# Two output stores cut into 119 and 9 rows, in place of own tiles for the halves of each w_in block and an earlier near half of the first mask

## The chip, the cores and the metric

The kernel runs on one core of one Trainium2 chip. The metric is the device time of one execution in microseconds (us), from the median of three runs. The core's engines are called PE (matrix products, with PEld for its weight loads), DVE (vector), ACT (activation), POOL (general purpose) and SP (which only issues DMAs). DMAs issued on one queue are carried out by 16 DMA engines side by side.

## The reference

Two stages follow each other, both with a recurrence over 768 steps of each of 4 sequences. The first is gated linear attention with 8 heads of width 48; its output, heads side by side (384 wide), is the input of the second, a gated state space block with inner width 512.

```python
for t in range(S):                       # first stage, per batch and head
    state = alpha[t][:, None] * state + outer(k[t], v[t])
    y[t] = q[t] @ state
x = heads_side_by_side(y)                # (4, 768, 384)

proj = x @ w_in                          # second stage; w_in is 384 x 1024
val, gate = proj[..., :512], proj[..., 512:]
for t in range(S):
    h = exp(A_log) * h + val[:, t];  ys[:, t] = h
out = (silu(gate) * ys) @ w_out          # w_out is 512 x 384
```

The weights and `A_log` come as 64-bit floats and are turned into 32-bit floats on the chip; the other inputs are 32-bit floats.

## The kernel before

The work is cut into 12 groups of 256 steps (3 groups for each of the 4 sequences), each of two chunks of 128. In a chunk the recurrence of the first stage becomes products of matrices: with running products of alpha (a scan on DVE, `products`, for the first group `chunk_products`), q is multiplied by the running product and k by its inverse (`Z`), the scores are k by q (`scores`), they are masked to the causal half (`masks`), multiplied with v (`values`), and what came from earlier chunks is added (`carried`, with the state that `state` sums up from the transposed keys of `keys`). `join` puts the heads side by side as `xT` by DMAs. The second stage projects a group in four blocks (`project`: for each block of 128 inner rows, three products for the value and three for the gate), runs the recurrence as a scan on DVE (`hidden`), gates it (`gate`, ACT and POOL), and multiplies with w_out (`output`).

The order is written out by hand: every engine runs its instructions in the order in which the program text gives them, and a framework adds the waits, by what each tile is written and read by. The group loop interleaves the second stage of group n with the first stage of group n+1 and the scans of group n+2; the first two groups have a longer prologue of their own (lines 849 to 982).

These places matter here:

- **Masks.** The scores of a chunk lie in two PSUM banks, one for even heads ("near") and one for odd heads ("far"). `masks_near` (L734) multiplies the near half with the mask on DVE; `masks_far` copies the far half on ACT (L729) and masks the copy on POOL (L730). The pair of banks comes in turn from one tile that spans two banks (`both`, b23) and from two tiles of one bank each (b4, b5). In b23, whichever of L734 and L729 stands second in the program waits for the first one; in b4 and b5 neither waits for the other.
- **Prologue.** `masks(0, 0, True)` puts the near half of the first chunk's mask ahead of the copy of the far half. Later, for group 1, the order on PE is scores(1,0), keys(1,0), scores(1,1), keys(1,1), state(1,0), values. The pair b23 goes to scores(1,0), the pair b4, b5 to scores(1,1).
- **Weights.** A w_in block is loaded by two DMAs (value half, gate half), each into its own tile `bits_in[i][vg]`. `low_word` (ACT, L531) turns the low 32-bit words into integers, `high_word` (DVE, L540 and L542) puts together the high words, and `word_sum` (POOL, L548) adds both into `w_in[i][vg]`, half by half. `check_w` (DVE, L559) finds the largest and smallest high word of each half, for a check whose outcome `fast` returns; if it is bad, a general kernel runs after the fast one.
- **Last stores.** In the last group both output tiles are copied from PSUM by DVE (L841) and stored by SP (L842), 128 rows of 1536 bytes each. After them the program branches over the general kernel (L1058) and ends.

Of the kernel before, what the change touches and what calls it, by code (L numbers as in the profile page):

```python
# [10 lines left out]
FP32 = mybir.dt.float32  # L11
U8 = mybir.dt.uint8
U32 = mybir.dt.uint32
AF = mybir.ActivationFunctionType
ALU = mybir.AluOpType
# [322 lines left out]
I32 = mybir.dt.int32  # L338
# [8 lines left out]
def fast(  # L347
# [18 lines left out]
    nc = tc.nc  # L366
    B, H, S, D = q.shape
    DM = H * D
    DI = moe_A_log.shape[0]
    C = 128  # L370
    G = 2
    GC = G * C
    NG = S // GC
    N = B * NG
    NT = GC // 32
    NK = DM // C
    NI = DI // C
# [6 lines left out]
    const = pool("const", 1)  # L384
# [3 lines left out]
    p4 = pool("p4", 4)  # L388
# [4 lines left out]
    next_mm, next_pair = itertools.cycle("016"), itertools.cycle((0, 1))  # L393
# [52 lines left out]
                             in_=v[b, :, ds(g * GC + c * C, C), :].rearrange("h p d -> p h d"))  # L446


    w_in = [[const.tile([C, NK, C], FP32, name=f"w_in{i}{vg}") for vg in range(2)] for i in range(NI)]
    w_out = const.tile([C, NI, DM], FP32, name="w_out")  # L450
    NW = NI + 2
    bits_in = [[const.tile([C, NK, C, 2], U32, name=f"bits_in{i}{vg}") for vg in range(2)] for i in range(NI)]
    bits_out = const.tile([C, NI, DM, 2], U32, name="bits_out")

    def load_w_in(i, engine):
        for vg in range(2):
            engine.dma_start(out=bits_in[i][vg].rearrange("p kk n two -> p kk (n two)"),
                             in_=moe_w_in.bitcast(U32)[:, ds(2 * (vg * DI + i * C), 2 * C)]
                             .rearrange("(kk p) n -> p kk n", p=C))

# [28 lines left out]
    inv_c = [inv[:, ds(c * 4 * C, 4 * C + 1)] for c in range(G)]  # L489
    ratio = const.tile([C, N, 4], FP32, name="ratio")  # L490
    above = const.tile([C, N], FP32, name="above")
    wmin = const.tile([C, NI + NW], FP32, name="wmin")
    wmax = const.tile([C, NI + NW], FP32, name="wmax")
    ok = const.tile([C, 4], FP32, name="ok")
    flag = const.tile([1, 1], I32, name="flag")

# [19 lines left out]


    def unit(i):

        if i < NI:  # L520
            return list(zip(bits_in[i], w_in[i]))
        return [(bits_out[:, 2 * (i - NI) + r, None], w_out[:, 2 * (i - NI) + r, None]) for r in range(2)]

    wrs = {}

    def low_word(i):
        wrs[i] = []
        for bits, w in unit(i):
            _, x, y = w.shape
            wr = p4.tile([C, x, y], I32, tag=f"wr{len(wrs[i])}", name="wr")  # L530
            nc.scalar.activation(wr, bits[..., 0], AF.Copy, scale=2.0 ** -29)  # L531
            wrs[i].append(wr)

    def high_word(i, banks):

        for (bits, w), bank in zip(unit(i), banks):
            _, a, n = w.shape
            x = bank[:, 0:NK] if a == NK else bank.rearrange("p h n -> p (h n)")[:, None, 0:n]
            h = bits[..., 1]
            nc.vector.tensor_scalar(out=x, in0=h, scalar1=3, scalar2=0x3FFFFFFF,  # L540
                                    op0=ALU.logical_shift_left, op1=ALU.bitwise_and)
            nc.vector.scalar_tensor_tensor(out=w.bitcast(U32), in0=h, scalar=0xC0000000, in1=x,  # L542
                                           op0=ALU.bitwise_and, op1=ALU.bitwise_or)

    def word_sum(i):
        for (_, w), wr in zip(unit(i), wrs.pop(i)):
            w = w.bitcast(I32)
            nc.gpsimd.tensor_tensor(out=w, in0=w, in1=wr, op=ALU.add)  # L548

    def check_w(i):  # L550
        his = []
        if i < NI:
            his = [t.rearrange("p kk n two -> p (kk n) two")[:, :, 1].bitcast(FP32) for t in bits_in[i]]
        else:
            his = [bits_out[:, ds(2 * (i - NI), 2)].rearrange("p cc n two -> p (cc n) two")[:, :, 1].bitcast(FP32)]
        for half, hi in enumerate(his):
            j = 2 * i + half if i < NI else NI + i
            for t, op in ((wmax, ALU.max), (wmin, ALU.min)):
                nc.vector.tensor_reduce(out=t[:, j:j + 1], in_=hi, axis=mybir.AxisListType.X, op=op,  # L559
                                        apply_absolute_value=True)  # L560
                if half == len(his) - 1:
                    yield

    def check_end():
        red = const.tile([C, 4], FP32, name="red")
# [56 lines left out]
    def chunk_products(c, al):  # L622

        by_place = lambda t: t.rearrange("p (h n) -> p h n", h=4)
        al_0, flat = by_place(al)[:, :, 0], last_c[c].rearrange("p h n -> p (h n)")[:, 0:4 * C]
        prod, inv = prod_c[c], inv_c[c]
        nc.vector.tensor_mul(first_c[:, :, 0], al_0, ends[-1])  # L627
        nc.vector.memset(al_0, 0.0)
        nc.vector.tensor_tensor_scan(out=prod, data0=al, data1=first_c.rearrange("p h n -> p (h n)"),
                                     initial=0.0, op0=ALU.mult, op1=ALU.max)  # L630
        yield
        end, inv_end = by_place(prod)[:, :, C - 1], last_c[c][:, 1:5, 0]
        ends.append(end)
        if c:
            nc.vector.tensor_scalar(out=ratio[:, 0], in0=end, scalar1=1.0 / FIRST_PRODUCT, scalar2=None,
                                    op0=ALU.mult)
        nc.vector.reciprocal(inv_end, end)
        nc.vector.tensor_copy(out=inv[:, 4 * C:], in_=last_c[c][:, 4, 0:1])
        nc.vector.tensor_tensor_scan(out=inv[:, 0:4 * C][:, ::-1], data0=al[:, ::-1], data1=flat[:, ::-1],
                                     initial=last_c[c][:, 4, 0:1], op0=ALU.mult, op1=ALU.add)  # L640
        yield
# [56 lines left out]
    def keys(m, c, b=None):  # L698

        if (m % NG) * G + c == NG * G - 1:  # L700
            return
        tp = mm(4, C, b=b)
        for p in range(4):
            nc.tensor.transpose(tp[:, p, :], Zs[m][:, p, 1, ds(c * C, C)], ident)
        nc.scalar.activation(ktms[c].rearrange("p a i d -> p a (i d)"), tp, AF.Copy)

    def scores(m, c):
        Z = Zs[m]
        cols = ds(c * C, C)
        sc = pair_of(4, C)  # L710
        for p in range(4):
            for i in range(2):
                rows = ds(64 * i, D)
                nc.tensor.matmul(sc[i][:, p, :], Z[rows, p, 1, cols], Z[rows, p, 0, cols], start=True, stop=True)  # L714
        As[m, c] = p2.tile([C, 2, 4, C], FP32, tag="A", name="A"), sc

    def masks(m, c, near_first=False):
        if near_first:
            masks_near(m, c)
        masks_far(m, c)  # L720
        if not near_first:
            masks_near(m, c)

    def mask_all():
        return mask[:, None, :].to_broadcast([C, 4, C])
# [1 line left out]
    def masks_far(m, c):  # L727
        A, sc = As[m, c]
        nc.scalar.activation(A[:, 1], sc[1], AF.Copy)  # L729
        nc.gpsimd.tensor_mul(A[:, 1], A[:, 1], mask_all())  # L730

    def masks_near(m, c):
        A, sc = As[m, c]
        nc.vector.tensor_mul(A[:, 0], sc[0], mask_all())  # L734
# [59 lines left out]
    def project(n, cc):  # L794
        if cc == 0:
            fs[n] = p1.tile([C, NI, GC], FP32, tag="f", name="f")
        xT = xTs[n]
        pv, pg = mm(GC), mm(GC)
        for vg, pj in enumerate((pv, pg)):
            for kk in range(NK):  # L800
                nc.tensor.matmul(pj, w_in[cc][vg][:, kk, :], xT[:, kk, :],  # L801
                                 start=(kk == 0), stop=(kk == NK - 1))
        return pv, pg

# [19 lines left out]
    def output(n):  # L824
        b, g = divmod(n, NG)
        os = [mm(DM) for c in range(G)]

        def part(ccs):
            for c in range(G):
                for cc in ccs:  # L830
                    nc.tensor.matmul(os[c], fs[n][:, cc, ds(c * C, C)], w_out[:, cc, :],  # L831
                                     start=(cc == 0), stop=(cc == NI - 1))

        def finish():
            part(range(split, NI))
            for c in range(G):
                o_sb = p3.tile([C, DM], FP32, tag="o_sb", name="o_sb")
                if n < N - 1:
                    nc.scalar.activation(o_sb, os[c], AF.Copy)  # L839
                else:  # L840
                    nc.vector.tensor_copy(out=o_sb, in_=os[c])  # L841
                nc.sync.dma_start(out=out[b, ds(g * GC + c * C, C), :], in_=o_sb)  # L842

        split = NI - 1 if n else NI // 2
        part(range(split))
        return finish
# [47 lines left out]
    qk[0]()  # L894
    qk[1]()
    scores(0, 0)
    steps = chunk_products(1, als[1].rearrange("p h n -> p (h n)"))
    next(steps)
    masks(0, 0, True)
    keys(0, 0, "6")  # L900
    al = both()
    for c in range(G):
        turned("a", 1, c, al.rearrange("p b (h n) -> p (b h) n", n=GC)[:, :, ds(c * C, C)])
# [28 lines left out]
    qk.append(natural_qk(1, "q", 1, mm(4, C, b="6")))  # L932
    next(steps)
    qk[0]()
    scores(1, 0)
    masks_far(1, 0)
    keys(1, 0, "0")
    qk[1]()
    qk[2]()
    masks_near(1, 0)  # L940
    scores(1, 1)
    masks(1, 1)
    keys(1, 1, "1")
    next(next_pair)
    low_word(0)
    state(1, 0)
    values(1, 0)
# [142 lines left out]
```

## Time and profile before

| | us |
|---|---|
| median of 3 runs (295.08 to 296.49) | 295.79 |
| the profiled execution's own time | 295.08 |
| its span, first to last instruction | 293.4 |
| PE busy in the span | 281.5 |
| DVE busy | 224.7 |
| POOL busy | 116.4 |
| ACT busy | 100.3 |

Times in profile lines are microseconds from the start of the span unless marked ns. In a timeline line the first number is the start, the second the busy time, then engine, line of the kernel, operation, what is written and read, sizes, the number of merged instructions, and in brackets the idle time of the engine ahead of it and what ended that. "SPq" marks DMA issues by SP. A group line that merges instructions gives the time from its first start to its last end. In DMA answers a row of 40 digits or of 40 GB/s values cuts the window into 40 equal slices. On PE each 32-bit product shows as two records, so the 24 products of a projection are 48.

### The profile page before, as it was taken

Reading aid. Unit: us, or ns where it says so; the run is one execution under the profiler, and the core shown is the slowest. Engines: PE = TensorE matmul, PEld = TensorE weight load, DVE = VectorE, ACT = ScalarE, POOL = GpSimd, SP = SyncE. Lnnn points to the kernel's source line nnn. Section 1 sums busy time; section 2 is a strip of 40 time slices with the busy share of each in tenths; the row PEclk is TensorE's granted clock in tenths of the full one; section 3 lists DMA queues with packets and bytes.
Section 4 is the critical chain, followed back from the end, with each engine's and each line's share of the span. In section 5 each row is a group of like instructions: output and inputs, shape, how many; then the busy total and the mean of one; then the engine's idle time right before and its main releaser. Section 6 shows DMA issues by size and latency. Waiting matters only on the chain. (4 is left out here: it accounts for less than half of the span.)

```text
span 293.4 us, 6146 instructions
## 1 busy us (share of the span) xinstructions
PE 281.5 (96%) x2345; PEld 226.5 (77%) x2345; DVE 224.7 (77%) x277; ACT 100.3 (34%) x226; POOL 116.4 (40%) x116
## 2 busy tenths in 40 slices
PE   7699999999999999999999999999999999999992
PEld 6578877885886896886886886886886886886870
DVE  5998887899996799799699699699699695312211
ACT  2457634432432432432432431431531531431110
POOL 7138791374642612642613513542523423401110
PEclk9999999999999999999999999999999999999998
DMA  9999969999992991991991991891891401101101
GB/s 129 163 162 298 366 125 169 233 264 212 237 207 65 236 167 34 246 187 35 244 175 34 241 185 34 219 202 37 210 213 39 108 11 35 54 11 31 55 4 63
DMA packets 71231, 42.09 MB, mean 143 GB/s; under 512 B 47492, under 2 KB 70536, under 8 KB 71192
## 3 DMA queue, kind: packets, MB, share of 16 engines
q1 hardware_dynamic: 69760, 40.96, 67.3%
q0 software_dynamic: 384, 0.44, 0.7%
q8 instruction: 20, 0.33, 0.6%
q10 hardware_dynamic: 1048, 0.20, 0.4%
q14 instruction: 19, 0.16, 0.2%
HBM read 33.33 MB, written 4.72 MB: 130 GB/s over the span
## 5 line engine op out<-in xcount | busy, mean ns | idle before, releaser
L801 PE MATMUL mm<-xT,w_in 128*128 128x256 f32 x576 | 131.0, 383 | 0.0
L801 PEld LDWEIGHTS mm<-xT,w_in 128*128 128x128 f32 x576 | 107.4, 190 | 17.8 <-issue 1.9
L817 POOL TENSOR_TENSOR f<-sg,hh 128x256 f32<-128x256 f32 x48 | 62.0, 1291 | 94.9 <-DVE hh L809 45.7
L831 PE MATMUL mm<-w_out,f 128*128 128x384 f32 x192 | 64.6, 487 | 0.7 <-DVE hh L809 0.6
L730 POOL TENSOR_TENSOR A<-A,mask 128x512 f32<-128x512 f32 x24 | 30.1, 1271 | 66.7 <-ACT A L729 66.7
L831 PEld LDWEIGHTS mm<-w_out,f 128*128 128x128 f32 x192 | 36.2, 190 | 24.1 <-DVE hh L809 1.3
L816 ACT ACTIVATE sg<-mm 128x256 f32<-128x256 f32 x48 | 18.4, 383 | 91.6 <-PE mm L801 89.5
L809 DVE TENSOR_TENSOR_SCAN hh<-a_dec,hh,mm 128x256 f32<-128x256 f32 x32 | 23.2, 726 | 20.2 <-PE mm L801 20.1
L734 DVE TENSOR_TENSOR A<-pair,mask 128x512 f32<-128x512 f32 x24 | 16.1, 688 | 26.6 <-ACT A L729 16.9
L661 DVE TENSOR_TENSOR_SCAN prod<-aT,first 128x1024 f32<-128x1024 f32 x10 | 27.5, 2750 | 0.1
L682 DVE TENSOR_TENSOR_SCAN inv<-aT,last 128x1025 f32<-128x1025 f32 x10 | 25.5, 2548 | 0.3
L839 ACT ACTIVATE o_sb<-mm 128x384 f32<-128x384 f32 x22 | 10.8, 490 | 43.8 <-PE mm L831 43.8
L714 PE MATMUL pair<-Z 48*128 48x128 f32 x384 | 25.2, 279 | 0.5 <-DVE first L627 0.2
L714 PEld LDWEIGHTS pair<-Z 48*128 48x128 f32 x384 | 22.6, 187 | 2.9 <-issue 2.1
L745 PE MATMUL pair<-A,v 128*64 128x128 f32 x352 | 21.3, 274 | 0.0
L745 PEld LDWEIGHTS pair<-A,v 128*64 128x64 f32 x352 | 19.1, 137 | 0.0
L647 DVE STREAM_TRANSPOSE aT<-raw_a 128x1024 f32<-128x1024 f32 x9 | 18.4, 2042 | 0.8 <-DMA raw_a<-in_alpha_dram 0.8
L647 DVE STREAM_TRANSPOSE Z<-raw_q 128x1024 f32<-128x1024 f32 x9 | 18.2, 2020 | 0.0
L647 DVE STREAM_TRANSPOSE Z<-raw_k 128x1024 f32<-128x1024 f32 x9 | 18.2, 2020 | 0.0
L729 ACT ACTIVATE A<-pair 128x512 f32<-128x512 f32 x24 | 13.3, 596 | 6.5 <-PE pair L714 3.5
L766 PEld LDWEIGHTS st<-v,ktm 128*64 128x64 f32 x320 | 11.4, 137 | 3.5 <-issue 3.5
L618 ACT ACTIVATE junk<-raw_a,minus 128x1024 bf16<-128x1024 f32 (+1 forms) x12 | 13.1, 1091 | 0.1
(119 smaller groups left out, 252.1 us busy)
## 6 DMA issues: line engine op xcount, KB each, us to landing
raw_k<-in_k_dram SPq DMA_DIRECT2D x24, 192.0 KB, 5.3
raw_q<-in_q_dram SPq DMA_DIRECT2D x24, 192.0 KB, 6.4
v<-in_v_dram SPq DMA_DIRECT2D x24, 192.0 KB, 6.4
out_dram<-o_sb SPq DMA_DIRECT2D x24, 192.0 KB, 1.9
raw_a<-in_alpha_dram SPq DMA_DIRECT2D x23, 192.0 KB, 4.2
raw_a<-in_alpha_dram SPq DMA_DIRECT2D x18, 176.0 KB, 4.3
raw_k<-in_k_dram SPq DMA_DIRECT2D x18, 176.0 KB, 5.7
raw_q<-in_q_dram SPq DMA_DIRECT2D x18, 176.0 KB, 6.7
```

The lines of the kernel that those rows point to most:

```text
L647: nc.vector.transpose(out=to.rearrange("p h (c j) -> p h j c", j=NT), in_=raw_bufs[m % NR][name].rearrange("p h (j d) -> p h j d", d=D)[:, ...
L661: nc.vector.tensor_tensor_scan(out=prod, data0=al, data1=first.rearrange("p h n -> p (h n)"), initial=0.0, op0=ALU.mult, op1=ALU.max)
L682: nc.vector.tensor_tensor_scan(out=inv[:, ::-1], data0=aT[:, ::-1], data1=lasts[:, 0:4 * GC + 1][:, ::-1], initial=0.0, op0=ALU.mult, op1= ...
L714: nc.tensor.matmul(sc[i][:, p, :], Z[rows, p, 1, cols], Z[rows, p, 0, cols], start=True, stop=True)
L730: nc.gpsimd.tensor_mul(A[:, 1], A[:, 1], mask_all())
L734: nc.vector.tensor_mul(A[:, 0], sc[0], mask_all())
L745: nc.tensor.matmul(ys[m][i][ds(64 * s, 64), e, ds(c * C, C)], v_sb[:, c, 2 * p + i, :], A[:, i, p, :], start=(c == 0 and e == 0), stop=Fal ...
L801: nc.tensor.matmul(pj, w_in[cc][vg][:, kk, :], xT[:, kk, :], start=(kk == 0), stop=(kk == NK - 1))
L809: nc.vector.tensor_tensor_scan(out=hh, data0=a_dec[:, cc:cc + 1].to_broadcast([C, GC]), data1=pv, initial=prev_h[cc][:, GC - 1:GC] if n % ...
L816: nc.scalar.activation(sg, pg, AF.Silu)
L817: return lambda: nc.gpsimd.tensor_mul(fs[n][:, cc, :], sg, hhs.pop((n, cc)))
L831: nc.tensor.matmul(os[c], fs[n][:, cc, ds(c * C, C)], w_out[:, cc, :], start=(cc == 0), stop=(cc == NI - 1))
```

## The change

Four edits, all in `fast`.

1. `w_in[i]` and `bits_in[i]` become one tile for both halves of a block, with the half as the third dimension. `low_word` is one ACT instruction of 128x768 in place of two of 128x384 (it then waits for both DMAs of the block), as it is for the two parts of w_out. `high_word` and `word_sum` stay two halves, but the DVE instruction for the first half now waits for both DMAs too. `check_w` makes two reductions of 128x768 for each block in place of four of 128x384.
2. In chunk (0,0) the copy of the far half stands ahead of the near half in the program. In the built program L734 of this chunk then waits for L729 (before, L729 waited for L734), and the transposes of alpha of group 1 (L592), which reuse the pair of banks, wait for L734 in place of L729. The order of instructions on each single engine is the same here.
3. In group 1 the pair of banks is swapped (`next(next_pair)` stands earlier), and keys(1,0) moves behind scores(1,1): PE has scores(1,0), scores(1,1), keys(1,0), keys(1,1); ACT has both copies of far halves, then both copies of keys. Now L734 of chunk (1,1), in place of that of (1,0), waits for its L729. No DMA is moved.
4. Each of the two stores of the last group becomes two, of 119 rows and of 9 rows, issued one after the other on SP.

```diff
-    w_in = [[const.tile([C, NK, C], FP32, ...) for vg in range(2)] for i in range(NI)]
+    w_in = [const.tile([C, NK, 2, C], FP32, name=f"w_in{i}") for i in range(NI)]
-    bits_in = [[const.tile([C, NK, C, 2], U32, ...) for vg in range(2)] for i in range(NI)]
+    bits_in = [const.tile([C, NK, 2, C, 2], U32, name=f"bits_in{i}") for i in range(NI)]
...
     def low_word(i):
-        wrs[i] = []
-        for bits, w in unit(i):
-            _, x, y = w.shape
-            wr = p4.tile([C, x, y], I32, tag=f"wr{len(wrs[i])}", name="wr")
-            nc.scalar.activation(wr, bits[..., 0], AF.Copy, scale=2.0 ** -29)
-            wrs[i].append(wr)
+        lo, _, w = unit(i)
+        _, x, y, z = w.shape
+        wrs[i] = p4.tile([C, x, y, z], I32, tag="wr", name="wr")
+        nc.scalar.activation(wrs[i], lo, AF.Copy, scale=2.0 ** -29)
...
     def word_sum(i):
-        for (_, w), wr in zip(unit(i), wrs.pop(i)):
-            w = w.bitcast(I32)
-            nc.gpsimd.tensor_tensor(out=w, in0=w, in1=wr, op=ALU.add)
+        w, r = unit(i)[2].bitcast(I32), wrs.pop(i)
+        for half in range(2):
+            x, y = (t[:, :, half] if i < NI else t[:, half] for t in (w, r))
+            nc.gpsimd.tensor_tensor(out=x, in0=x, in1=y, op=ALU.add)
...
-                nc.sync.dma_start(out=out[b, ds(g * GC + c * C, C), :], in_=o_sb)
+                rows = [C] if n < N - 1 else [119, 9]
+                for i, size in enumerate(rows):
+                    at = sum(rows[:i])
+                    nc.sync.dma_start(out=out[b, ds(g * GC + c * C + at, size), :], in_=o_sb[ds(at, size)])
...
     scores(0, 0)
+    masks_far(0, 0)
+    keys(0, 0, "6")
     steps = chunk_products(1, als[1].rearrange("p h n -> p (h n)"))
     next(steps)
-    masks(0, 0, True)
-    keys(0, 0, "6")
+    masks_near(0, 0)
...
     qk[0]()
+    next(next_pair)
     scores(1, 0)
     masks_far(1, 0)
-    keys(1, 0, "0")
     qk[1]()
     qk[2]()
     masks_near(1, 0)
     scores(1, 1)
     masks(1, 1)
-    keys(1, 1, "1")
-    next(next_pair)
+    keys(1, 0, "1")
+    keys(1, 1, "0")
     low_word(0)
     state(1, 0)
```

## The prediction

> **What bounds the kernel now.** I read the page first, then busy time by stage, then the timelines of the prologue and of the stretch after it, engine by engine, and last the end of the span with its DMAs. The page's busy row and two stages of the stage table:
>
> ```profile
> PE 281.5 (96%) x2345; PEld 226.5 (77%) x2345; DVE 224.7 (77%) x277; ACT 100.3 (34%) x226; POOL 116.4 (40%) x116
> ...
> 47.00:75.00 28.00, 27.32 (x239) 22.07 (x238) 26.76 (x29) 10.32 (x23) 12.12 (x14) 1.00 1.10 227
> 75.00:97.00 22.00, 22.00 (x185) 17.81 (x184) 17.42 (x17) 7.59 (x19) 9.71 (x6) 1.00 0.76 168
> 252.00:274.00 22.00, 22.00 (x164) 17.48 (x160) 5.59 (x17) 5.09 (x13) 5.40 (x6) 1.00 0.10 32
> ```
>
> From 75 us on PE is busy for all of each stage (22.00 of 22.00, at full clock, 1.00), so a delay of PE that still stands at 75 us stands at the end, and nothing that only DVE, ACT or POOL save after 75 us counts. Before 75 us PE has small gaps, and after its last product (287.5) come 5.9 us of copying, storing and closing. The change touches these two places only. First the prologue, timelines of DVE, ACT and PE:
>
> ```profile
> 12.26 0.69 DVE L734 TENSOR_TENSOR A<-pair,mask 128x512 f32<-128x512 f32 x1
> 12.98 0.60 ACT L729 ACTIVATE A<-pair 128x512 f32<-128x512 f32 x1 [3.04 <-DVE A L734]
> ...
> 23.47 0.68 DVE L607 TENSOR_TENSOR Z<-mm,prod 128x512 f32<-128x512 f32 x1
> 24.99 0.69 DVE L734 TENSOR_TENSOR A<-pair,mask 128x512 f32<-128x512 f32 x1 [0.84 <-ACT A L729]
> ...
> 24.78 1.16 PE L714 MATMUL pair<-Z 48*128 48x128 f32 x16
> 26.45 0.67 PE L766 MATMUL st<-v,ktm 128*64 128x48 f32 x16
> 30.29 0.92 PE L801 MATMUL mm<-xT,w_in 128*128 128x256 f32 x3
> ```
>
> From 12.26 to 24.15 DVE runs back to back, and PE's scores follow its Z products; PE's first projection starts at 30.29. Then the last gap of PE:
>
> ```profile
> 55.52 2.06 DVE L647 STREAM_TRANSPOSE aT<-raw_a 128x1024 f32<-128x1024 f32 x1 [0.82 <-DMA raw_a<-in_alpha_dram]
> 67.56 0.68 DVE L809 TENSOR_TENSOR_SCAN hh<-a_dec,hh,mm 128x256 f32<-128x256 f32 x1
> ...
> 65.56 2.10 PE L831 MATMUL mm<-w_out,f 128*128 128x384 f32 x6
> 68.30 3.49 PE L831 MATMUL mm<-w_out,f 128*128 128x384 f32 x10 [0.64 <-DVE hh L809]
> ```
>
> At 55.52 DVE waits for a load, then runs back to back until the scan at 67.56, and PE's second output product waits for that scan's bank. This gap is set by a DMA and DVE, not by PE. Now the end:
>
> ```profile
> 287.49 1.03 SPq L842 DMA_DIRECT2D out_dram<-o_sb  x2
> ...
> DMA  0000000559872988501110000000010200000000
> DMA packets 293, 0.44 MB, mean 69 GB/s; under 512 B 32, under 2 KB 288, under 8 KB 288
> q1 hardware_dynamic: 288, 0.39, 17.4%
> q14 instruction: 4, 0.03, 1.7%
> q8 instruction: 1, 0.02, 1.4%
> out_dram<-o_sb SPq DMA_DIRECT2D x2, 192.0 KB, 3.3
> ...
> DMA packets 20, 0.03 MB, mean 17 GB/s; under 512 B 3, under 2 KB 20, under 8 KB 20
> ...
> DMA to landing us min/median/max: 1.9/1.9/6.5
> ```
>
> In the window 287 to 293.4 there are 256 rows and 32 small packets (one closing count for each of 16 engines and each store). Two bursts, then a trickle: from 290.0 on (second packet line) only 17 rows and 3 counts are left, so at most two engines are late. Code is fetched in the same stretch (q8, q14). The two stores land after 3.3 us where the median store takes 1.9. A row takes 0.174 x 16 x 6.4 / 288 = 0.062 us.
>
> **The change, part by part.** The sum is made against the profiled execution, 295.08 (span 293.4 and 1.7 around it); the median of the runs is 0.71 above it.
>
> *First mask.* ACT's L729 can start once the scores are there: PE's L714 of 16 records takes 1.16 from 10.99, so 12.15, and in the prologue ACT follows PE by 0.10: 12.25 to 12.85. L734 then starts at 12.88 in place of 12.26: +0.62 on DVE, and its queue behind it is full: the scans, the Z products of chunk (0,1) and of group 1. PE's transposes (L592, 13.68) wait for L734's end, 13.57, in place of L729's, 13.58: no change. The scores after them follow DVE, and scores(1,0) starts at 23.72 in place of 23.10. The far half is finished on POOL 0.7 earlier, which nobody waits for.
>
> *Keys behind the second scores.* Scores(1,1) now stands right behind scores(1,0), and waits for the last Z product, 24.15 + 0.62 = 24.77: it starts at 24.92 (24.78 before). With L714 taking 1.09 to the next start, keys(1,0) runs 26.01 to 26.67, ACT copies it 26.76 to 27.36, and state(1,0) starts at 27.43 in place of 26.45. So PE is +0.98 late, of it 0.36 from this move; the rest of its chain (0.51 + 1.76 + 0.55 + 1.02 to L801) is unchanged: first projection 31.27. DVE's near masks, 25.0 and 26.8, are ready in time; the words of block 0 on POOL end at about 29.9 and 31.0, needed at 31.3 and 32.6.
>
> *Merged tiles.* One 128x768 low word, by the nearest row (L618, 128x768) 0.93, where two of 0.56 took 1.03. The first sum starts at most 0.4 later than its half alone would, behind slack of over 1 us. Waiting for both halves' DMAs costs up to 1.13 us for block 2 (ACT waited until 30.92 and 32.05), but DVE takes that block only behind the scan at 32.87. The join of group 1 slips 0.4 on ACT; its DMAs queue behind the loads anyway, as they land at 39 to 41 us and are needed at 47. POOL with rows of 128 apart: the nearest pair, L921 (such rows) 1.28 against L730 1.27, so nothing. The reductions: 16 x 0.53 become 8 x 0.93, DVE saves 1.0 us after 75 us, under PE: nothing.
>
> *What is late next.* PE carries +0.98 from 30.3 to 66.5. DVE's chain from 55.5 does not: it waits there for a load that queues behind other loads, and with +0.98 its previous scan ends at 55.67, 0.15 after that load. L734 of group 2 then waits for a later L729 (57.5 to 58.1), but before, L658 took 0.99 beside POOL's mask, which moves to 58.15; the scan at 67.56 comes no later. PE reaches its second output product at 66.54 + 1.94 = 68.48, and no longer waits, against 68.30: 0.8 of the 0.98 is taken up. At 72.7 another 0.1 goes (scores there waited for DVE's Z). Front: +0.1, bounded by -0.4 (a PE delay of only half the size with a DVE chain that gets shorter) and by +1.0 (nothing taken up).
>
> *Last stores.* SP issues four times 0.33 in place of two; the second 119 rows can be issued at 288.22, as before (288.19). How many engines 119 rows use, the trace does not show. It shows equal shares: 128 rows on 16 engines, and on ACT's queue 1048 packets, which is 1024 rows of a load with its 16 counts and a 4-row transfer with 4. Equal shares of 119 (7 x 17) mean 7 engines with 17 rows, or one; of 9, nine engines or three. I take 7 and 9, and the same engines each time, which is the slower way. Data starts 0.84 after issue: 17 rows from 288.32 end at 289.37, the next 9 at 289.43, the second 17 at 290.5, the last 9 at 290.55. An undisturbed store has 1.9 - 0.84 - 8 x 0.062 = 0.56 from last row to landing: 291.1, against 288.19 + 3.2 = 291.4. That is -0.3 if the late engines are not among the seven. If one is, it has 36 rows where it had 16: +1.2. If 119 rows go over 16 engines, 0 to +0.2. All on one engine: 238 x 0.062, +12, excluded by me as no transfer here does so.
>
> The Trainium skill, page "DMA: Bandwidth & Descriptors", section "Why a DMA increments its semaphore by 16 and not by 1", says that such a transfer uses the largest number of engines up to 16 that divides its rows, and the lowest-numbered ones; the counts above agree as far as they go, and which numbers they are, no row shows. By it 7 and 9 are right, and both stores share the first seven.
>
> Against the change stands, on the same page under "Rules for kernel authors", that two transfers of disjoint partitions share the engines and should be one: by it the sum of this edit is 0 or worse. The row (two late engines of 16) weighs more here; the page's "Latency and other measured facts" has engines 7 and 15 as the usually slow ones, which would leave the seven free and give -0.3.
>
> Sum: +0.1 - 0.3 = -0.2 against 295.08, so 295.6 on the scale of the median. Against a noise bound of 0.5% (1.5 us, about what a measurement can tell) that is no change.
>
> **Rivals.** *Late engine among the seven* (slower): the code fetch sits on an engine that now has 36 rows. For it: seven of 16 engines get everything, and fetches at the end are certain. Against: only two engines are late. Price +1.2 and +0.1 of the front, 297.1; it is over the bound if the rows hold up the fetches too (the same window gives 1.4% x 16 x 6.4 = 1.4 us for q8's, 0.4 for each of q14's), up to 298. It decides once the slow engine's rows end later than 290.9.
> *Front not taken up* (slower): if loads slip with PE, the gap at 67 stays, +1.0 - 0.3: 296.5. For it: several loads wait for buffers. Against: DVE's wait at 55.52 is for a load, not PE.
> *Nothing splits*: 119 rows still spread over all engines; the change does not do what it says to the end of the store. 296.0.
> *Gain larger* (faster): the median run is 0.7 above the profiled one; if that is the late engines, it goes too: 295.6 - 0.7 = 294.9, with the front at its lower bound 294.4. For it: the late engines vary with fetches. Against: nothing shows what the other runs lost.
>
> **How the numbers follow.** Chances: forecast 0.40, late engine 0.28, front 0.12, nothing splits 0.06, larger gain 0.14. Slower by over 0.5%: two thirds of the late engine, half of the front, some of the rest, 0.28. Faster: most of the larger gain and a seventh of the forecast, 0.20. Within: 0.52. Range 294.2 to 297.8, which leaves out the far ends of the first and last rival; the forecast's own range is 294.8 to 296.4.
>
> **What would show it.** In the changed profile: L734 at about 12.9 with a wait for L729; L801's first product at about 31.3; no PE gap at 67 to 68; PE busy throughout after 75, its last product within 0.3 us of 287.5; four stores, all landed by 291.1 without a trickle. Wrong if PE's end is 0.5 us off, or the last rows come after 291.

## The result and the profile after

The changed kernel takes 296.87 us (median), the kernel before in the same comparison 296.01: the ratio, which goes by all twenty runs of each and not by the two medians, is 1.0038 with a 95% interval of 1.0024 to 1.0052. The change costs about 1.1 us, where a gain of 0.2 us was forecast. The time lies inside the forecast's range and inside the 0.5% that was called no change, but the kernel became slower and not faster, and the interval leaves out 1. The profiled execution took 296.88 us with a span of 295.1 (before: 295.08 and 293.4).

First the stages, in the page's busy row and in the stage table of the changed kernel (window, length, then busy time and count of PE, PEld, DVE, ACT and POOL, granted clock, DMA share, GB/s):

```profile
PE 281.5 (95%) x2345; PEld 226.8 (77%) x2345; DVE 224.9 (76%) x269; ACT 99.3 (34%) x220; POOL 113.5 (38%) x116
...
47.00:75.00 28.00, 28.00 (x243) 22.61 (x241) 27.30 (x31) 11.00 (x25) 11.10 (x14) 1.00 1.16 229
75.00:97.00 22.00, 22.00 (x184) 17.69 (x184) 18.10 (x18) 7.57 (x19) 7.72 (x6) 1.00 0.75 162
252.00:274.00 22.00, 22.00 (x168) 17.63 (x165) 5.76 (x17) 5.43 (x13) 5.39 (x6) 1.00 0.12 36
```

PE's gap between 47 and 75 us is gone (28.00 of 28.00 where it was 27.32), and later stages are full as before. The loss is therefore in the prologue, as far as it is not taken up, or behind PE's last product. The prologue, timelines of DVE, POOL and PE:

```profile
12.90 0.69 DVE L734 TENSOR_TENSOR A<-pair,mask 128x512 f32<-128x512 f32 x1 [0.58 <-ACT A L729]
13.51 0.74 DVE L638 TENSOR_SCALAR ratio<-prod 128x4 f32<-128x4 f32 x1
...
14.44 1.27 DVE L642 TENSOR_TENSOR_SCAN inv<-mm,last 128x512 f32<-128x512 f32 x1
...
12.95 1.27 POOL L730 TENSOR_TENSOR A<-A,mask 128x512 f32<-128x512 f32 x1 [7.00 <-ACT A L729]
...
24.19 2.27 PE L717 MATMUL pair<-Z 48*128 48x128 f32 x32 [0.17 <-DVE Z L610]
27.79 0.67 PE L766 MATMUL st<-v,ktm 128*64 128x48 f32 x16 [0.31 <-ACT ktm L708]
31.62 2.64 PE L801 MATMUL mm<-xT,w_in 128*128 128x256 f32 x11
...
66.78 5.32 PE L831 MATMUL mm<-w_out,f 128*128 128x384 f32 x16
71.94 1.04 PE L707 MATMUL mm<-ident,Z 128*128 128x128 f32 x8
```

The same places in the kernel before, where the prediction does not show them:

```profile
12.87 0.16 DVE L635 TENSOR_SCALAR ratio<-prod 128x4 f32<-128x4 f32 x1
...
13.21 1.27 DVE L639 TENSOR_TENSOR_SCAN inv<-mm,last 128x512 f32<-128x512 f32 x1
...
13.74 1.28 POOL L730 TENSOR_TENSOR A<-A,mask 128x512 f32<-128x512 f32 x1 [7.79 <-ACT A L729]
...
71.63 1.04 PE L704 MATMUL mm<-ident,Z 128*128 128x128 f32 x8
```

DVE's near mask is 0.64 later (12.26 before), as forecast. But the small operation behind it, on 4 numbers per partition, takes 0.74 us where it took 0.16, and it ends at 14.25, just when POOL's mask of the far half ends (14.22). So DVE's second scan starts 1.23 late, and PE's first projection 1.33 late (30.29 before; 0.98 was forecast). At 66.78 the six and ten products of L831, which had a gap of 0.64 between them, run as sixteen without one, and at 71.94 only 0.31 of the 1.33 is left (L704 at 71.63 before).

Now the end. The next two fences show the DMAs of the 6.5 us that begin with DVE's first copy of the last output (287.24, before 286.90), as the busy share of the 16 engines in 40 slices of 0.16 us, and SP's waits in the last 8 us (in all, times, longest). First the changed kernel, then the one before:

```profile
DMA  1000003024563433544554544310000000010001
...
q1 hardware_dynamic: 288, 0.39, 20.8%
...
287.82 1.47 SPq L845 DMA_DIRECT2D out_dram<-o_sb  x4
...
SPq L1062 <- SPq L1062: 3.6, 2, 3.1
```

```profile
DMA  0000000519982699531110000000010100000000
...
q1 hardware_dynamic: 288, 0.39, 17.2%
...
SPq L1058 <- SPq L1058: 2.5, 2, 2.0
```

Before, the rows come in two bursts at 9 tenths and a thin trickle. After, the same 288 packets (256 rows and 32 closing counts) fill a little under half of the engines (4 and 5 of 10) for 3 us: that is seven engines of 16. And SP, which has branched over the general kernel and has only its closing waits left, stands 3.1 us without a releaser in place of 2.0.

PE ends at another time in each profiled execution, so tails are compared from the start of DVE's first last copy. The table was read from the records of semaphores, DMA packets and branches of all the profiles that follow (us after that copy's start). The packets of q8 (16 KB) and q14 (8 KB), queues that the profile marks "instruction", are called code packets here. "Code packet" in the table is the start of the q14 packet after which SP goes on; that this packet is SP's is inferred from the steady 1.5 to 1.7 us between the two (1.9 with the keys late, where SP waited for a landing). "Last row" is the start of the last row.

| last two stores | SP branches | code packet | last row | last landing | span end |
|---|---|---|---|---|---|
| before | 1.67 | 2.80 | 3.99 | 4.50 | 6.45 |
| changed kernel | 2.11 | 4.22 | 5.09 | 5.71 | 7.91 |
| front alone, whole stores | 1.67 | 3.11 | 3.50 | 4.10 | 6.68 |
| far half first, whole stores | 1.67 | 2.73 | 4.11 | 4.62 | 6.57 |
| keys late, whole stores | 1.67 | 2.75 | 4.58 | 5.10 | 7.05 |
| 119 and 9 alone | 2.09 | 4.26 | 5.13 | 5.76 | 7.95 |
| changed, small operations first | 2.11 | 4.24 | 5.10 | 5.72 | 7.91 |
| 119 on SP, 9 on ACT | 1.62 | 4.60 | 5.05 | 5.74 | 8.14 |
| 115 and 13 | 2.89 | 4.84 | 5.62 | 6.75 | 8.55 |
| 112 and 16 | 4.31 | 5.48 | 5.49 | 6.54 | 9.31 |
| 127 and 1 | 10.30 | 11.39 | 17.85 | 18.36 | 20.13 |
| no branch, whole stores | none | none | 2.75 | 3.17 | 4.29 |
| no branch, 119 and 9 | none | none | 4.46 | 4.98 | 5.98 |
| stores in the Else, whole | -11.28 | earlier | 3.37 | 3.79 | 4.92 |

Of the 1.8 us between the two profiled executions 1.46 are in this tail (7.91 against 6.45) and 0.34 ahead of it. Tails vary too: the four with whole stores and a branch behind them end at 6.45 to 7.05, the three with all four stores of 119 and 9 on SP at 7.91 to 7.95, on average 1.2 apart, which fits the 1.1 us of all runs. In the kernels with a branch at the end, the span ends 1.8 to 1.95 us behind the last landing or 3.5 to 3.85 behind the code packet, whichever is later. Before, both give 6.45; in the changed kernel the landing alone would give 7.66 and the code packet gives 7.9.

One more packet bears on the cause. The first q14 packet after the end of the last copies (1.26) is taken for DVE's, which branches at 0.72 in all these kernels with a branch behind the stores. It starts at 2.28 to 2.30 with whole stores, at 2.42 with 112 and 16, at 3.24 to 3.32 with 119 and 9, at 3.06 with 115 and 13, and at 1.98 with 127 and 1. No edit moved that branch, so rows on seven or five engines made this code 0.8 to 1.0 us late by themselves.

### The profile page after: what moved, and what is told of

It reads as the page before. It is cut to its first block, busy times and chain, and to the rows that moved or that the text cites. A ratio compares the mean times of both kernels' runs of the same rounds, so it can differ in the third digit from the quotient of the medians.

```text
span 295.1 us, 6128 instructions
## 1 busy us (share of the span) xinstructions
PE 281.5 (95%) x2345; PEld 226.8 (77%) x2345; DVE 224.9 (76%) x269; ACT 99.3 (34%) x220; POOL 113.5 (38%) x116
## 5 line engine op out<-in xcount | busy, mean ns | idle before, releaser
L801 PE MATMUL mm<-xT,w_in 128*128 128x256 f32 x576 | 131.1, 384 | 0.0
L801 PEld LDWEIGHTS mm<-xT,w_in 128*128 128x128 f32 x576 | 107.3, 190 | 18.0 <-issue 2.0
L817 POOL TENSOR_TENSOR f<-sg,hh 128x256 f32<-128x256 f32 x48 | 58.9, 1228 | 96.4 <-DVE hh L809 48.6
L831 PE MATMUL mm<-w_out,f 128*128 128x384 f32 x192 | 64.4, 487 | 0.0
L831 PEld LDWEIGHTS mm<-w_out,f 128*128 128x128 f32 x192 | 36.2, 190 | 23.1 <-POOL w_out L555 0.6
L734 DVE TENSOR_TENSOR A<-pair,mask 128x512 f32<-128x512 f32 x24 | 16.1, 688 | 27.5 <-ACT A L729 17.7
L664 DVE TENSOR_TENSOR_SCAN prod<-aT,first 128x1024 f32<-128x1024 f32 x10 | 28.1, 2810 | 0.1
L729 ACT ACTIVATE A<-pair 128x512 f32<-128x512 f32 x24 | 13.3, 597 | 6.6 <-PE pair L717 5.3
L766 PE MATMUL st<-v,ktm 128*64 128x48 f32 x320 | 13.0, 224 | 0.3 <-ACT ktm L708 0.3
```

The lines of the kernel that those rows point to most:

```text
L766: nc.tensor.matmul(st[ds(64 * i, 64), p, :], ktms[c][:, p, i, :], vs[m % NV][:, c, 2 * p + i, 0:D], start=(ch == 0 and p == 0), stop=(ch = ...
L801: nc.tensor.matmul(pj, w_in[cc][:, kk, vg, :], xT[:, kk, :], start=(kk == 0), stop=(kk == NK - 1))
L817: return lambda: nc.gpsimd.tensor_mul(fs[n][:, cc, :], sg, hhs.pop((n, cc)))
```

## The experiments

**Which part carries the loss?** The changed kernel with whole stores, and the kernel before with cut ones:

```diff
-                rows = [C] if n < N - 1 else [119, 9]
-                for i, size in enumerate(rows): ...
+                nc.sync.dma_start(out=out[b, ds(g * GC + c * C, C), :], in_=o_sb)
```

> The changed kernel with its last two stores made whole again (128 rows each), so only the front's edits and the merged tiles are left. Theory 'rows' (the tail carries the loss: what counts is how many rows the busiest DMA engine holds): PE's end 0.34 us late as in the changed kernel (first last copy 287.24 against 286.90), last landing about 291.7, ratio to before 1.000 to 1.002. Rival 'front' (the front carries the loss): the whole of it stays, ratio about 1.0035 to 1.004. Rival 'issues' (four issues on SP in place of two make its branch, and the code after it, late): as 'rows' here.

```diff
-                nc.sync.dma_start(out=out[b, ds(g * GC + c * C, C), :], in_=o_sb)
+                rows = [C] if n < N - 1 else [119, 9]
+                for i, size in enumerate(rows):
+                    at = sum(rows[:i])
+                    nc.sync.dma_start(out=out[b, ds(g * GC + c * C + at, size), :], in_=o_sb[ds(at, size)])
```

> The kernel before with only the last two stores cut into 119 and 9 rows. Theory 'rows': seven engines hold 17+1+17+1 = 36 rows of 0.065 us in place of 16; PE's end as before (286.90), last landing about 292.6 against 291.40, ratio 1.003 to 1.005. Rival 'front': ratio 1.000. Rival 'issues': 1.003 to 1.005 too.

The front alone: ratio 1.0001 (0.9981 to 1.0020), first last copy at 287.00 (286.90 before). The cut stores alone: 1.0032 (1.0011 to 1.0053), span end 7.95 us after the first last copy. The two waits of SP, first of the front alone, then of the cut stores alone:

```profile
SPq L1059 <- SPq L1059: 2.8, 2, 2.3
```

```profile
SPq L1061 <- SPq L1061: 3.7, 2, 3.2
```

The rival "front" falls. The tail carries the loss, and the three edits of the front together move nothing that can be measured (the interval is 0.2% to either side). One expectation missed: PE's end in the second run came 1.48 us later than expected, with a front that is that of before. In that execution DVE waited 2.28 us for the load of raw_a in place of 0.82, and PE carried the difference to the end:

```profile
56.98 2.06 DVE L647 STREAM_TRANSPOSE aT<-raw_a 128x1024 f32<-128x1024 f32 x1 [2.28 <-DMA raw_a<-in_alpha_dram]
```

So one profile's PE end says little below 1.5 us, and only differences inside one trace, or medians, can be used there.

**Rows or issues?** The same cut with other sizes, again on the front of before. 112 rows go to 16 engines (7 each), 115 to 5 (23 each), as the landings on the semaphores show (16, and 5 beside one that comes at once); both have four issues.

```diff
-                rows = [C] if n < N - 1 else [119, 9]
+                rows = [C] if n < N - 1 else [112, 16]      # and [115, 13] in the second
```

> The kernel before with the last two stores cut into 112 and 16 rows: four issues as in the changed kernel, but every engine holds 7+1+7+1 = 16 rows, as before. Theory 'rows': the second large part is issued 0.1 us later than the second store before, last landing 291.4 to 291.6, ratio 1.000 to 1.001. Rival 'issues': SP's branch 0.4 to 0.8 us later and with it everything behind it, ratio 1.002 to 1.005, the same as with 119 and 9 rows.

> The kernel before with the last two stores cut into 115 and 13 rows: 115 is 5 times 23, so by equal shares five engines hold 23+1+23+1 = 48 rows. Theory 'rows': 12 rows of 0.065 us, 0.8 us, later than with 119 and 9: last landing about 293.4, ratio 1.006 to 1.008. Rival 'issues': the same ratio as with 119 and 9. If parts are not shared out equally, the ratio is that of 112 and 16.

112 and 16 gave 1.0049 (1.0024 to 1.0073), the "issues" number and not that of "rows". But the trace shows another cause than the one named in that rival. DMA answer for the 6.5 us from the first last copy, and SP's timeline, of 112 and 16:

```profile
DMA  0000000019996210000000000049985202000000
...
288.88 3.68 SPq L845 DMA_DIRECT2D out_dram<-o_sb  x4
```

The rows are quick here (two bursts at 9 tenths), but there are 2.5 us between them: SP's third issue, at 289.79, took 2.29 us where the others take 0.35 to 0.43. A 16 KB code packet of queue q8 ran from 289.87 to 291.72, and the issue ended 0.36 us after it. The tail of this execution is 2.9 us longer than that of before, the median of the twelve runs only 1.8 us longer (297.73 against 295.90), so the usual wait may be shorter. With 115 and 13 the fourth issue took 1.12 us and ended 0.37 after the q8 packet (290.13). The same is seen in the kernel before under its load bursts: of the 21 issues from 45 us on that overlap a q8 packet in its trace, eight end 0.37 to 0.39 us after that packet's end. Of issues in a row that meet a packet, the first often passes, and the one behind it stands. So the two more issues are not free: besides their 0.33 each there is the chance of standing behind a code packet. How often one stands, these traces do not show. In the changed kernel none of the four issues stood (0.27 to 0.37 each).

115 and 13 gave 1.0053 (1.0029 to 1.0078). Its last row came 0.49 us later than with 119 and 9 (5.62 against 5.13) and its last landing 0.99 later, where 0.8 was expected of 12 more rows; the span ended only 0.6 later, and the ratio is under the 1.006 to 1.008 of "rows". Held issue and rows are mixed in it, so this run does not decide alone.

**One engine.** The clean form of the rows' cost:

```diff
-                rows = [C] if n < N - 1 else [119, 9]
+                rows = [C] if n < N - 1 else [127, 1]
```

> The kernel before with the last two stores cut into 127 and 1 rows. 127 is a prime: by equal shares one engine takes all of it, 256 rows of 0.065 us in all, 16.6 us in place of 1.0. Theory 'rows': last landing some 16 us after the first last copy in place of 4.5, span end 13 to 15 us later, ratio 1.045 to 1.05; if the code fetch of DVE and SP lies on that engine too, it comes late as well. If parts are spread over all engines whatever their rows: as with 112 and 16, ratio about 1.005.

Ratio 1.0438 (1.0386 to 1.0491). 256 rows followed each other singly from 1.39 to 17.85 us after the first last copy, 0.064 each. GB/s in 40 slices of its first 6.5 us:

```profile
GB/s 0 0 0 0 0 0 0 0 9 19 0 110 69 28 19 9 9 19 9 9 28 19 28 28 19 28 79 19 28 28 19 28 28 19 28 28 19 28 28 19
```

A steady 19 to 28 GB/s is one engine (the two peaks are code packets). So a store is shared out in equal parts over the largest number of engines, up to 16, that divides its rows. The Trainium skill says this on the page "DMA: Bandwidth & Descriptors", section "Why a DMA increments its semaphore by 16 and not by 1", and gives 127 rows as an example; the run agrees. SP's code packet started 1.09 us after its branch here, while that engine had rows for another 6.5 us, without a gap between them when the packet ran: the code does not come over it. Its branch was late (10.30), as two of the four issues stood for 2.41 and 6.49 us; the longer one ended at 10.25, just before the first store landed (10.35). What they waited for is not shown.

**Late branch, or rows?** The rows as in the change, on the front of before, but only two issues on SP; the minus line stands for the cut stores of above:

```diff
-                    nc.sync.dma_start(...)
+                    (nc.scalar if i else nc.sync).dma_start(...)
```

> The kernel before with the last two stores cut into 119 and 9 rows, and the 9 rows issued by ACT in place of SP. SP branches 1.7 us after the first last copy starts, as before, in place of 2.1, and the rows are spread as in the changed kernel. If the two more issues on SP carry the loss (late branch): SP's fetch starts 1.1 to 1.4 us after its branch, ratio about 1.000. If the rows on seven engines carry it: SP's fetch still starts some 2.1 us after its branch, span end 7.4 to 7.6 us after the first last copy (6.5 before, 7.9 with four issues on SP), ratio about 1.002 to 1.004.

Ratio 1.0059 (1.0033 to 1.0085), span end 8.14 us after the first last copy. SP's issues and wait:

```profile
288.52 0.98 SPq L845 DMA_DIRECT2D out_dram<-o_sb  x2
...
SPq L1061 <- SPq L1061: 4.3, 2, 3.8
```

SP branches as early as before (1.62), yet its code packet starts 2.98 us after the branch, where it is 1.13 before. "Late branch" falls: the rows on seven engines hold the code up, as DVE's packet says too (3.24 in place of 2.29). It is worse than the 7.4 to 7.6 expected. ACT now branches late too (1.62 in place of -3.90) and fetches code at the same time (two packets, at 4.51 and 4.60, of which the second is taken for SP's); that this is the reason was not tested.

**The tail without the branch.** These two leave out the general kernel and the branch to it (the flag is still worked out):

```diff
-    with tc.If(good <= 0):
-        general(tc, *args)
```

> The kernel before without the conditional call of the general path behind the fast one (the flag is still worked out and read, but no engine branches on it, and the general path is left out). Theory 'fetch' (the end is set by the code that SP fetches after its branch: it goes on 1.5 to 1.7 us after that fetch starts, and the span ends 3.6 to 3.8 us after it starts): no fetch is left at the end, SP's closing waits run straight up to the last landing and the span ends 1.9 us behind it; if the fetches also made two engines late, the last landing is 3.2 us rather than 3.9 us after the first last copy, or earlier, ratio 0.994 to 0.999. Rival 'landing' (the end is set by the last landing alone, which the branch does not touch): ratio 1.000.

> The kernel before without the conditional call of the general path, and with the last two stores cut into 119 and 9 rows. Theory 'fetch': the part of the loss that comes from SP's late branch and the delayed fetch (some 0.4 us of it the branch) goes, what stays is the rows' own landing on seven engines: span end 0.8 to 1.3 us later than in the version without branch and with whole stores, where with the branch it is 1.4 us. Rival 'landing': the same 1.4 us.

Whole stores: 0.9912 (0.9877 to 0.9948); 119 and 9: 0.9967 (0.9939 to 0.9995). DMAs of the 6.5 us from the first last copy, first whole, then cut:

```profile
DMA  0000000019992799400000000000000000000000
...
out_dram<-o_sb SPq DMA_DIRECT2D x2, 192.0 KB, 1.9
```

```profile
DMA  0000000024544534454545344320000000000000
...
q1 hardware_dynamic: 288, 0.39, 20.6%
```

Two things follow. Without code packets no engine is late: the trickle is gone, the stores land after 1.9 us in place of 3.3, and the tail is 2.2 us shorter. So the end of the kernel before was set by code, not by the stores as such. The gain is larger than expected (0.994 to 0.999), and the general kernel went with the branch, so the two are not told apart here (the version with the stores in the Else, below, keeps it). And the cut still costs 1.7 us here (5.98 against 4.29), more than the 0.8 to 1.3 expected, all of it in the landing (4.98 against 3.17). So neither theory had it whole: the rows on seven engines are enough for the loss, and in these tails the code fetch adds nothing to it (1.5 us with the branch, 1.7 without; the ratios say 0.3 to 0.4% with it and 0.55% without, with intervals too wide to tell these apart). 36 rows on an engine should take 36 x 0.065 = 2.3 us; from the first to the last row it was 3.08. 37 rows of this kernel took over 0.09 us, up to 0.4, 29 of them in the first 1.1 us of the first store and 8 where the second begins; with whole stores and no branch not one did. With 112 and 16, on all 16 engines but beside code packets, 61 did. Why rows are slow behind a cut, no run shows.

**The prologue.** Two edits alone, on the kernel before, and one more on the changed kernel that takes the small DVE operations out of POOL's way:

```diff
+    masks_far(0, 0)
+    keys(0, 0, "6")
     steps = chunk_products(1, als[1].rearrange("p h n -> p (h n)"))
     next(steps)
-    masks(0, 0, True)
-    keys(0, 0, "6")
+    masks_near(0, 0)
```

> The kernel before with only the first mask's order changed (far half copied and keys transposed first, near half behind the scan on DVE). By the prediction's sum DVE slips by 0.62: second scan (13.21 before) at 13.85, scores of group 1 (23.10) at 23.7, first projection (30.29) at 30.9. If POOL's multiplication, now beside DVE's small operations, holds one of them up (0.74 in place of 0.16), second scan at 14.4, scores of group 1 at 24.2, first projection at 31.3. The time itself stays within 0.3% of before.

```diff
+    next(next_pair)
     scores(1, 0)
     masks_far(1, 0)
-    keys(1, 0, "0")
 ...
-    keys(1, 1, "1")
-    next(next_pair)
+    keys(1, 0, "1")
+    keys(1, 1, "0")
```

> The kernel before with only the keys of group 1 behind the second scores, in one pair of banks. By the prediction's sum: scores of group 1 at 23.10 as before, state of group 1 (26.45) 0.3 to 0.4 late, first projection (30.29) at 30.6 to 30.7. If it costs nothing by itself, 30.3; if the whole +1.33 of the changed kernel came from here, 31.6. The time itself stays within 0.3% of before.

```diff
         nc.vector.tensor_copy(out=inv[:, 4 * C:], in_=last_c[c][:, 4, 0:1])
+        yield
 ...
     next(steps)
+    next(steps)
     masks_near(0, 0)
```

> The changed kernel with DVE's three small operations of the second scan (ratio, reciprocal, copy) put ahead of the near half of the first mask, into the time in which DVE waits for ACT. If it was POOL's multiplication beside them that made the first of them 0.74 us: it takes 0.16 again, the second scan starts at 13.6 in place of 14.44, scores of group 1 at 23.4 in place of 24.19, first projection at 30.8 to 31.0 in place of 31.62. If the length has another cause it stays 0.74 and nothing moves. Either way the loss in the tail is that of the changed kernel: span end 7.7 to 8.1 us after the first last copy.

The far half first, alone (DVE and PE; this execution's first scan starts 0.13 earlier than before's, so 0.13 is to be added to compare):

```profile
13.37 0.74 DVE L635 TENSOR_SCALAR ratio<-prod 128x4 f32<-128x4 f32 x1
...
14.30 1.27 DVE L639 TENSOR_TENSOR_SCAN inv<-mm,last 128x512 f32<-128x512 f32 x1
...
31.24 1.99 PE L801 MATMUL mm<-xT,w_in 128*128 128x256 f32 x8
```

The changed kernel with the small operations first:

```profile
12.35 0.17 DVE L638 TENSOR_SCALAR ratio<-prod 128x4 f32<-128x4 f32 x1
...
13.50 1.27 DVE L643 TENSOR_TENSOR_SCAN inv<-mm,last 128x512 f32<-128x512 f32 x1
...
30.69 2.64 PE L802 MATMUL mm<-xT,w_in 128*128 128x256 f32 x11
...
12.95 1.27 POOL L731 TENSOR_TENSOR A<-A,mask 128x512 f32<-128x512 f32 x1 [7.00 <-ACT A L730]
```

The far half first brings the 0.74 us with it and puts the first projection 1.08 late (31.37 against 30.29). With the small operation ahead of POOL's mask, which stays where it was, it takes 0.17, the scan starts 0.94 earlier and the first projection 0.93 earlier (30.69 against 31.62). So the operation did wait for POOL, and in the changed kernel it ended at 14.25, 0.03 us after POOL's mask. The Trainium skill has the rule: page "SBUF — State Buffer", section "Who interferes with whom", says that of a DVE operation in a mode that reads one operand through two ports and a POOL operation the first holds the other off for its whole instruction. The trace agrees with the blocking; in which mode the operation ran, it does not show. The keys alone:

```profile
30.40 2.86 PE L801 MATMUL mm<-xT,w_in 128*128 128x256 f32 x12
```

With 0.14 to be added the first projection is 0.25 late, where 0.36 was forecast and 0.3 to 0.4 expected. The two edits together make 1.33, all that the changed kernel has. The times of these three single runs were 295.23, 295.88 and 295.95 against 296.09 of before: no difference that one run could show, the last of them less than the tail's cost (its tail is 7.91, but PE's end came early, at 286.31). Merged tiles were not run alone.

**A version that beats both.** If code after the branch sets the end, the branch should come before the last work. The last copies and stores go into the Else of the conditional call; everything is still computed, and the general kernel, which must leave the last outputs' two PSUM banks alone, has one buffer in place of three in one of its pools.

```diff
     with tc.manual_schedule():
-        good = fast(tc, *args)
-    with tc.If(good <= 0):
+        good, last = fast(tc, *args, last_ps, last_sb)
+    with tc.If(good <= 0) as bad:
         general(tc, *args)
+    with bad.Else():
+        last()          # the two copies L841 and stores L842
 ...
```

> The kernel before, whole, with the last copies and stores moved into the Else of the conditional call: every engine takes its branch before its last work (DVE and SP while PE is still at the last products), and the copies and the two whole stores run behind it. Theory 'fetch': DVE's and SP's code is fetched beside PE's products, no such fetch lies between the stores and the end, and the span ends 4.3 us (as without a branch) to 5.2 us (if PE's own fetch still makes one engine late) after the first last copy starts, in place of 6.5: ratio 0.991 to 0.996. Rival: the jump at the end of the Else fetches again, or the landing alone sets the end: ratio 0.999 to 1.001.

Ratio to before 0.9942 (0.9919 to 0.9964): 1.7 us faster, and faster than the changed kernel by more. DMAs of the 6.5 us from the first last copy, SP's issues and waits:

```profile
DMA  0000030019992000089930000000000000000000
...
q8 instruction: 1, 0.02, 0.9%
...
288.80 1.68 SPq L848 DMA_DIRECT2D out_dram<-o_sb  x2
...
SPq L1095 <- DMA out_dram<-o_sb: 0.5, 1, 0.5
```

SP's long wait without a releaser is gone; what it waits for is the store. The tail is 4.92 us, inside the expected 4.3 to 5.2. What is left above 4.29 is again a held issue: the second store's stands 1.11 us and ends 0.37 after the q8 packet (289.18 to 290.11).

## Why the prediction was wrong

- **What bounds the kernel**: right. PE is full from 75 us on, and the front's delay was measured where it still stood at 75 us.
- **First mask**: the wait was right (L734 at 12.90, forecast 12.88). Wrong was "The far half is finished on POOL 0.7 earlier, which nobody waits for": POOL's mask moved into the way of DVE's ratio operation, 0.16 became 0.74, and the step cost 1.1 us at the first projection in place of 0.62. The prediction had the same effect in hand further on ("L658 took 0.99 beside POOL's mask") and did not ask for it here. In the end it cost next to nothing, as the gap at 67 took most of it up.
- **Keys behind the second scores**: right in kind, 0.25 in place of 0.36.
- **Merged tiles**: 0.92 to 0.96 us for a 128x768 low word on ACT, as priced (0.93), and two sums on POOL in 2.12 to 2.13 (2.14 before). "Nothing" is borne out as far as the front as a whole shows it.
- **What is late next**: right. PE's gap at 67 took up most of it: 1.33 late at the first projection, 0.31 at 71.9, 0.21 at L801 behind it (74.90 against 74.69). Front +0.1 was forecast; the front alone gives a ratio of 1.0001.
- **Last stores**: this is the step that failed. Seven and nine engines, four issues of 0.27 to 0.37 and the start of data were right. The sum "An undisturbed store has 1.9 - 0.84 - 8 x 0.062 = 0.56 from last row to landing: 291.1" puts the landing 4.2 us after the first last copy; it was 5.71. The -0.3 also sets cut stores without late engines against whole stores with two of them. Whole stores without code packets land at 3.17, so by the sum's own terms the cut costs 1.0 and gains only if it frees the stores of the late engines; measured without code packets it costs 1.8 (4.98).
- The no-branch pair splits the 1.5 between 4.2 and 5.71. 0.8 is there without code packets too, because rows on seven engines do not follow each other at 0.062 (3.08 us for 36 rows; the 0.062 had also shared the time among the 32 closing counts, and undisturbed rows take 0.064). 0.7 comes with them, because one of the late engines is among the seven: of the seven engines of the first 119 rows, six landed by 3.62 and the last at 4.74, where without the branch all landed by 3.60; and a last engine sends single rows from 291.65 to 292.33, after the others are done.
- The rival "late engine among the seven" named that engine, and its 297.1 came near the 296.87 measured. In part this is luck: its +1.2 was 20 more rows on one late engine, and the cut costs as much where no engine is late. Its "if the rows hold up the fetches too" was right (code packets 1 us late). "Against: only two engines are late" counted engines, where one is enough.
- The step took the landing for what ends the run as well. In the changed kernel this makes 0.25 us (7.66 by the landing, 7.91 measured). In the trace of before, SP stood until 291.31 at the wait for a store that had landed at 290.94, so it was not waiting for data there; but its next wait ended 0.02 us after the second store's landing (291.40), so before the change the landing and the code gave the same end.
- **Noise**: 0.5% was called about what a measurement can tell. Twenty runs a side told 0.14% either way.
- **The skill's rules**: "Rules for kernel authors" on the page "DMA: Bandwidth & Descriptors", one transfer in place of two of disjoint partitions, was right here. "Latency and other measured facts" on that page, which has engines 7 and 15 as the usually slow ones, was the argument for -0.3. The prediction left out that the page ties this, as its best guess, to DMAs whose descriptors are made in software, and these stores go over a hardware queue ("q1 hardware_dynamic"). In this case one late engine is among the seven that a store of 119 rows uses. The page "Runtime: NRT & Kernel Launch", section "Instruction fetch mechanics", says that a taken branch to code outside the window waits for a fetch. The runs agree: 2.2 us of the tail of before go with the branch at its end.

## What to carry to other kernels

Leave the last store of a program whole, with a number of rows that 16 divides: 119 rows ran on seven engines, and 36 rows on each took 3.1 us where 16 on each of 16 took 1.3. Cutting it into 112 and 16, which 16 divides, lost time as well (1.0049). Compare like with like: a sum for an undisturbed version stands against the undisturbed version of before. Look at what an engine waits for behind its last DMA: where it stands at a wait that has been met, ask whether its code is late. Here a branch taken before the last work, with the last copies and stores behind it, gave back 1.7 us. And when an operation moves on one engine, look at what runs beside its new place: a POOL operation that nobody waited for cost DVE 0.58 us.

## What the runs showed of the hardware

- After a branch, SP's code packet (told by inference, as said above) starts 1.1 to 1.4 us later with rows on 16 engines, and SP goes on 1.5 to 1.7 us after that. With rows on seven engines the packet starts 2.1 to 3.0 us after the branch, with rows on five 1.95, with rows on one 1.1. DVE's moves from 2.3 to 3.3 with rows on seven.
- DMA issues on SP that stood beside a 16 KB code packet of q8 ended 0.36 to 0.39 us after that packet, eight of them in the trace of before and three at the end of other kernels: 2.29, 1.12 and 1.11 us for single issues, in place of 0.33.
- Rows of a store are mostly 0.062 to 0.065 us each on 16 engines and on one. On seven, 37 of 256 took over 0.09 without code packets and 38 with them; on 16 with whole stores none without them and 11 with them. What slows them stays open.
- Which engines carry code is open too, beyond this: of the two engines that are late beside code packets, one is used by a store over seven engines, and SP's code does not come over the one that a store of 127 rows uses.
